# Copies issued from ScalarE, first-product weights in two tiles, and preparation paced by estimated transfers, in a fused attention and expert kernel

## The chip, the cores and the metric

The kernel runs on one core of a Trainium2 chip. The metric is device time in microseconds (us); lower is better. A core has TensorE (PE, the matrix unit, with its weight loads shown apart as PEld), VectorE (DVE), ScalarE (ACT), GpSimd (POOL) and SyncE (SP, which only issues transfers and waits). Each runs its own list of instructions in order. Sixteen DMA engines move the data of all queues; a transfer is issued by an instruction on one engine's list, and if that instruction has to wait, everything behind it on that list waits too.

## The reference

Two blocks follow each other. First a lightning attention over 4 batches, 8 heads, 768 positions and 64 channels, in blocks of 64 positions with a decayed state; then a mixture of 4 experts over the 3072 tokens, all of them dense, with gates that are normalized probabilities.

```python
for b in range(nb):
    intra = np.einsum('bhic,bhjc->bhij', qb, kb) * Dmask[None]
    intra = np.einsum('bhij,bhjd->bhid', intra, vb)
    inter = np.einsum('bhid,bhde->bhie', qb * lam_pow[None], kv_state)
    out[:, :, sl] = intra + inter
    kv_state = lam_block[None, :, None, None] * kv_state + np.einsum('bhsd,bhse->bhde', kb_dec, vb)
...
p = domain_probs / (domain_probs.sum(-1, keepdims=True) + 1e-09)
for e in range(E):            # x is 3072 x 512, w1[e] 512 x 1024, w2[e] 1024 x 512
    h = np.maximum(x @ w1[e], 0.0)
    out += p[:, e:e + 1] * (h @ w2[e])
```

All data is float32.

## The kernel before

**Units and steps.** The tokens are worked in three groups of 1024, each with four experts, so there are twelve units (group, expert), listed in `units`. While the second product (`h @ w2`) of one unit runs, the first product (`x @ w1`) of the next one runs between its parts. Both products use Strassen's scheme with seven products, M1 to M7, in place of eight. In the first product each of the seven is split by the same scheme again, so one outer product consists of seven inner products of 128x256 matmuls. One pass of the inner loop (`for i in range(7)`) is called a step here: one outer product of the first product and one of the second. A step is cut into eight slots, and `now[0]` counts slots over the whole program. From unit 5 on (`NEST`) the second product is split twice too; these steps are called nested.

**Attention** of group 0 runs at the start. That of groups 1 and 2 is put between the steps by `attention`, at slots that `BEGIN` sets, from PSUM banks s0 and s1. The q and k chunks of the last third of the positions are not transposed by PE: they are first copied from DRAM to DRAM into the tensor `across` in 128 copies of 32 KB with rows of 32 floats (`bring_across`, L431 to L444). `trickle` issues one such copy per slot, and `load_more` issues at once what its batch still lacks, and then loads `qx` and `kx` from `across` (`load_across`).

**Weights.** A first product needs for every outer product its block of w1, or a sum of blocks, and the sums of its four quarters: seven pieces of 128x256. GpSimd makes these sums once per expert (`prepare_w1`, `inner_w1`, `inner`; for expert 1 `own_w1`), and SyncE stores the seven pieces, 896 KB, in the DRAM tensor `w1_ops`. For M1, M2 and M4 the block is a plain block of w1 (A11, A12, A22 in `A_OF`); for the other four it is a sum. `feed` (L928) reads the seven pieces back into one tile `ws_in` with a single transfer; two such tiles exist. It is called at the end of slot 0 of a step, of slot 4 in nested steps, for the first product of the next step. The operands of the second product are made alike: `prepare_w2` for units 0 to 4, `prepare_w2_ops` for the nested units, whose pieces go to `w2_ops` and come back in tiles `w2t`.

**What sets the order.** The engines' lists are written out by hand: everything is issued in the order in which this Python program runs. The preparation is a list of small pieces of work, `chores`. At the end of every slot `pump` starts the next one if the planner's clock `free` has come; this clock is pushed on by an estimate of GpSimd's time (`busy`), by a pace per token group (`PACE`), or by 7 slots once `spare` is set, at `NEST`. Stores go through `queue`, which lets them out some slots after the estimated end of their sums. `until` starts chores at once if something due isn't made yet. For each group after the first, `x_fill` loads the transposed activations of one outer product into its slot `xs`; four sums of them follow, on GpSimd (`x_inner`), or on VectorE for the last four of the seven outer products of the last group (`own_x`).

The names that the change and the prediction touch: `tt` L101, `load` L140, `store` L177, `pump` L187, `inner` L211, `prepare_w2_ops` L319, `x_fill` L387, `bring_across` L434, `trickle` L446, `load_across` L454, `feed` L928, `feed2` L1041, `feed3` L1107, `own_w1` L1421, `keep_own` L1438, and the loop over units and slots from L1628 on. Line L102 is the one line that all elementwise operations of VectorE and GpSimd share, L1018 the matmuls of the first product, L1072 and L1371 those of the second product (L1371 nested), L1026 and L1030 ScalarE's copies out of PSUM and its relu in the first product.

Of the kernel before, what the change touches and what calls it, by code (L numbers as in the profile page):

```python
# [21 lines left out]
def kernel(  # L22
# [30 lines left out]
    nc = tc.nc  # L53
# [46 lines left out]

    def tt(eng, o, a, b, op):  # L101
        eng.tensor_tensor(out=o, in0=a, in1=b, op=op)  # L102
        if eng is nc.gpsimd:
            busy[0] = max(busy[0], now[0]) + math.prod(o.shape[1:]) / (640 if spare else 480)
        else:
            vector(math.prod(o.shape[1:]), PSUM in (a.space, b.space))
# [6 lines left out]
    now, busy, free, filled, spare = [0], [0.0], [0.0], [0.0], []  # L113
# [31 lines left out]
    def load(n, names="qkv"):  # L145

        c, b = where(n)
        for name in names:
            x = ({"k": acc_tile, "v": w2_tile} if n < CPG else {}).get(name, small)(f"{name}n")
            src = {"q": q, "k": k, "v": v}[name][b, :, c * C:(c + 1) * C, :]  # L150
            if name == "v":
                to, of = x[:].rearrange("p (h d) -> p h d", d=D), src.rearrange("h p d -> p h d")
                for h in (slice(0, 4), slice(4, 8)) if n < CPG else (slice(0, 8),):
                    nc.sync.dma_start(out=to[:, h], in_=of[:, h])
# [20 lines left out]
    LEFT = 1  # L175
# [10 lines left out]
    def pump(pace=1.0, force=False):  # L186
# [5 lines left out]
        begins = chores and (force or free[0] <= now[0] and not (spare and busy[0] > now[0] + 1))  # L192
        while queue and (force or queue[0][0] <= now[0] or begins and len(queue) > LEFT):
            queue.pop(0)[1]()
        if begins:
            begin = free[0] = max(free[0], now[0] - 1)
            was = max(busy[0], now[0])
            chores.pop(0)()
            free[0] = max(free[0], begin + max(pace * (busy[0] - was), 7 if spare else 1))
# [11 lines left out]
    def inner(eng, what, to, blk, ops, at):  # L211
# [3 lines left out]
        for i, (name, x, y, op) in enumerate(ops):  # L215
            b[name] = s[:, SLOT[name]]
            tt(eng, b[name], b[x], b[y], op)
        store(lambda: (
            nc.sync.dma_start(out=to[:, 0], in_=blk[:, 0, 0:256]),
            nc.sync.dma_start(out=to[:, 1:5], in_=s[:]),  # L220
            nc.sync.dma_start(out=to[:, 5:7], in_=blk[:, 1].rearrange("p (a f) -> p a f", a=2)),
            made.add(what),
        ))
# [27 lines left out]
    def prepare_w1(e):  # L251
        st = {}

        def block(name, i, j):
            t = stage.tile([P, 2, W], FP32, name="w1b", tag="st")
            src = moe_w1[e, j * 256:(j + 1) * 256, i * W:(i + 1) * W]
            nc.sync.dma_start(out=t[:], in_=src.rearrange("(c p) f -> p c f", p=P))
            st[name] = t
# [15 lines left out]
    def prepare_w2(e):  # L274
        st = {}

        def block(name, i, j):
            t = stage.tile([P, 2, 2, DH], FP32, name="w2b", tag="st")
            for uu in range(2):
                for c in (slice(0, 1), slice(1, 2)) if e == 0 else (slice(0, 2),):  # L280
                    nc.sync.dma_start(out=t[:, uu, c], in_=w2_block(e, uu, i, j)[:, c])
            st[name] = t

        def total(name, n, a, b, op):
# [4 lines left out]
                nc.sync.dma_start(out=w2_sums[e, n].rearrange("p u w -> p (u w)"), in_=flat[0]),  # L289
# [17 lines left out]
    def inner_w2(e, m, blk, two):  # L307
# [8 lines left out]
        store(lambda: ([nc.sync.dma_start(out=to[:, x], in_=b[n]) for n, x in at], made.add(("w2", e, m))))  # L316

    def prepare_w2_ops(e, eased):
# [10 lines left out]
        def block(name, i, j):  # L329
            t = st[name] = two("w2b")  # L330
            for q in range(2):
                r = j * W + q * 256
                src = moe_w2[e, r:r + 256, i * DH:(i + 1) * DH]
                nc.sync.dma_start(out=t[q], in_=src.rearrange("(c p) d -> p c d", p=P))
# [53 lines left out]
    def x_fill(g, m):  # L388
# [3 lines left out]
        for a in range(2):  # L392
            nc.sync.dma_start(
# [3 lines left out]
        if g == LAST and SEQ.index(m) >= 3:  # L397
# [9 lines left out]
    def raw_w1(e, name):  # L407
# [6 lines left out]
        for c in range(2):  # L414
            r = j * 256 + c * P
            for f in (slice(0, 256), slice(256, W)) if e == 0 and i == 0 else (slice(0, W),):
                nc.sync.dma_start(out=to[c][:, f], in_=moe_w1[e, r:r + P, i * W:(i + 1) * W][:, f])
# [18 lines left out]
    def bring_across(b):  # L436
        for x, of in enumerate((q, k)):
            for y in range(4):
                for ac in range(NHP):
                    src = of[b, 4 * (y // 2) + ac, SECOND * C:, (y % 2) * 32:(y % 2 + 1) * 32]  # L440
                    to = across[x, y * 32:(y + 1) * 32, ac, b]
                    pieces.append((b, lambda to=to, src=src: nc.sync.dma_start(
                        out=to, in_=src.rearrange("(t p) d -> p t d", p=32),
# [10 lines left out]
    def load_across(n):  # L454
        c, b = where(n)
        for x, name in enumerate("qk"):
            t = small(f"{name}x")
            nc.sync.dma_start(
# [322 lines left out]
    def pair_sums(g, x, o):  # L781
# [3 lines left out]
        for to, a, b in ((0, b12, b11), (1, b22, s[:, 0]), (2, b22, b12), (3, b21, s[:, 1])):  # L785
            tt(nc.gpsimd, s[:, to], a, b, ALU.subtract)
        store(lambda: (
            nc.sync.dma_start(out=x_blocks[g - 1, :, x, 0], in_=b11),
            nc.sync.dma_start(out=x_blocks[g - 1, :, x, 1:3], in_=o[1][:].rearrange("p (i t) -> p i t", i=2)),
            nc.sync.dma_start(out=x_blocks[g - 1, :, x, 3:7], in_=s[:]),  # L790
# [137 lines left out]
    def feed(g, e, m):  # L928
        until(("w1", e, m))
        ws = stream.tile([P, 7, 256], FP32, name="ws_in", tag="w")  # L930
        nc.sync.dma_start(out=ws[:], in_=w1_ops[e, MS.index(m)])
        fed[g, e, m] = {i: ws[:, W1_AT[i]] for i in W1_AT}
# [109 lines left out]
    def feed2(g, e, m):  # L1042
# [3 lines left out]
        for uu in range(2):  # L1046
# [6 lines left out]
            nc.sync.dma_start(out=t[:], in_=src)  # L1053
# [3 lines left out]
    def second_product(g, e, m, banks):  # L1057

        def part(sj, s):
# [31 lines left out]
            if unit_of[g, e] in (E - 1, NEST - 1) and m in ("M2", "M6", "M5", "M3"):  # L1091
                to = rows[n] if g == 0 else partial[n % CPG * P:(n % CPG + 1) * P]
                results.append(lambda: nc.sync.dma_start(out=to[:, j * DH:(j + 1) * DH], in_=o))
# [16 lines left out]
    def feed3(e, m, k):  # L1110
# [3 lines left out]
        if e == FINAL and m != SEQ3[0]:  # L1114

            if k == 0:
                t = xp.tile([P, 7, 256], FP32, name="w2s", tag="x" + SEQ[SEQ3.index(m)])
                if (e, m) == PLAIN:
                    i, j = int(A_OF[m][1]) - 1, int(A_OF[m][2]) - 1
                    src = moe_w2[x_e, j * W:(j + 1) * W, i * DH:(i + 1) * DH]  # L1120
                    nc.sync.dma_start(out=t[:, 0:4], in_=src.rearrange("(k p) d -> p k d", p=P))
                    fed3[e, m, 0] = t
                    return
                nc.sync.dma_start(out=t[:], in_=w2_ops[x_e, MS.index(m)].rearrange("p k c d -> p k (c d)"))
# [5 lines left out]
        nc.sync.dma_start(  # L1130
# [59 lines left out]
    def give(m, t, tags, dds=(0, 1)):  # L1190
# [13 lines left out]
        nc.sync.dma_start(  # L1204
# [62 lines left out]
    def turned_product(t, h, w):  # L1267
# [10 lines left out]
        nc.sync.dma_start(  # L1278
# [12 lines left out]
    def first_result():  # L1291
# [14 lines left out]
        def park(x):  # L1306
            i, j = RESULT[x]
            to = parked[i * DH:(i + 1) * DH, j * W:(j + 1) * W].rearrange("(k p) t -> p k t", k=2)
            nc.sync.dma_start(out=to, in_=sums[x][:].rearrange("p (k t) c -> p k (t c)", k=2))

        def gather(n):
            t, po = small("y"), small("po")
            for b in range(4):
                c = n * P + b * 32
                nc.sync.dma_start(
# [3 lines left out]
            nc.sync.dma_start(out=po[:], in_=partial[n * P:(n + 1) * P])  # L1319
# [7 lines left out]
        def finish_rows(n):  # L1327
            t, po = gathered_out.pop(n)
            tt(nc.gpsimd, t[:], t[:], po[:], ALU.add)
            store(lambda: nc.sync.dma_start(out=rows[CPG + n], in_=t[:]))  # L1330
# [66 lines left out]
    b12.append(stream.tile([P, 7, 256], FP32, name="b12", tag="w"))  # L1397
# [23 lines left out]
    def own_w1(m):  # L1421
# [9 lines left out]
        )))  # L1431
# [5 lines left out]
    def keep_own(what, to, pieces):  # L1437
        return lambda: ([nc.sync.dma_start(out=to[:, x:y], in_=of) for (x, y), of in pieces], made.add(what))  # L1438
# [130 lines left out]
    fill = [(*u, m) for u in units[2:] for m in SEQ]  # L1569
# [59 lines left out]
    PACE = 1.0, 1.4, 1.0  # L1629
    first_steps = first_result()  # L1630
    for at, (g, e) in enumerate(units):
        if at == 0:
            chores.extend(prepare_w2(2) + prepare_w1(3) + prepare_w2(3))
            for x in (2, 3):
                chores.extend(prepare_w2_ops(x, False))
            chores.extend(prepare_w1(0))
            chores.extend(prepare_w2_ops(0, True))
# [6 lines left out]
        if at == NEST - 1:  # L1644
            forget()
        blocks, banks = {}, {}
        for i in range(7):
# [36 lines left out]
            for x, part in enumerate(order):  # L1684
# [31 lines left out]
                if x == (4 if nested else 0) and at * 7 + i >= 6 and fill:  # L1716
# [3 lines left out]
                if x % 2 or at * 7 + i >= 8:  # L1720
# [35 lines left out]
```

## Time and profile before

| | us |
|---|---|
| median of 3 runs | 1188.23 |
| lowest and highest | 1187.45, 1188.76 |
| profiled execution | 1193.83 |
| its span, first to last instruction | 1192.0 |

The page of the profile gives for each engine the time that it was busy, out of that span:

```profile
PE 1155.0 (97%) x8011; PEld 996.4 (84%) x8011; DVE 821.9 (69%) x1504; ACT 316.6 (27%) x638; POOL 802.9 (67%) x764
```

SyncE isn't in that line: issuing a transfer doesn't count as busy. What it does is read from the timeline of its queue (SPq), where each row is one issue or several of one line, with the time of its start and its length. The chain of work that ended last, followed back from the last instruction, is by engine and line:

```profile
PE 78%; DMA 8%; POOL 6%; DVE 5%; issue 2%; SPq 1%; ACT 1%; ACTq 0%; POOLq 0%; DVEq 0%
PE pg L1018 33%; PE pq L1371 20%; PE q L1072 15%; DMA ws_in<-w_ops 6%; POOL acc L102 2%; PE pM L1474 2%; POOL m L102 2%; PE pc L1474 2%; DVE m L102 2%; DVE sums L102 1%; DVE xs L102 1%; PE op L731 1%; PE sp L677 1%; POOL ops L102 1%; PE op L749 1%
```

The largest groups of transfers, with KB each and the median us from issue to landing:

```profile
ws_in<-w_ops SPq DMA_DIRECT2D x70, 896.0 KB, 6.9
w2t<-w_ops SPq DMA_DIRECT2D x129, 256.0 KB, 3.2
w2b<-in_moe_w_dram SPq DMA_DIRECT2D x56, 256.0 KB, 5.0
w_ops<-ops SPq DMA_DIRECT2D x28, 512.0 KB, 4.4
```

In such lines `pg` is the PSUM bank of the first product, `q` and `pq` those of the second, and numbers at the end of names are left out (`w_ops` stands for `w1_ops` and `w2_ops`). A wait is put down to what ended it.

### The profile page before, as it was taken

How to read it: one execution, taken by the hardware profiler on the slowest of the kernel's cores; microseconds unless marked ns; L12 is line 12 of the kernel's file. 1: busy time of each engine (PE TensorE's matmuls, PEld its weight loads, DVE VectorE, ACT ScalarE, POOL GpSimd, SP SyncE). 2: the span in 40 equal slices, each digit the busy share in tenths (PEclk: the TensorE clock that was granted, in tenths of full speed). 3: DMA queues.
4: the chain of work that ended last, by engine and by line, in shares of the span. 5: the costliest groups of instructions: out<-in, count | busy, mean ns of one | idle time of the engine just before them, and what ended most of it. 6: DMA issues, size and time to landing. Idle time of an engine off the chain costs nothing.

```text
span 1192.0 us, 21838 instructions
## 1 busy us (share of the span) xinstructions
PE 1155.0 (97%) x8011; PEld 996.4 (84%) x8011; DVE 821.9 (69%) x1504; ACT 316.6 (27%) x638; POOL 802.9 (67%) x764
## 2 busy tenths in 40 slices
PE   8999999989998899999999999999999999999998
PEld 7788888868777788887888888888888888888887
DVE  4576885568456766874775566798876576777785
ACT  3321122112211121121134242242253342241331
POOL 2846328545554486794689598798599794793894
PEclk9999999999999999999999999999999999999999
DMA  8884667889899999979786767686686967566642
GB/s 185 218 267 143 188 196 221 264 255 271 257 273 290 286 299 318 304 255 319 239 278 216 220 210 243 203 259 197 191 254 214 287 188 213 167 197 179 173 186 71
DMA packets 293994, 273.92 MB, mean 230 GB/s; under 512 B 139840, under 2 KB 240128, under 8 KB 293888
## 3 DMA queue, kind: packets, MB, share of 16 engines
q1 hardware_dynamic: 280096, 268.11, 73.9%
q10 hardware_dynamic: 13792, 4.41, 1.6%
q8 instruction: 64, 1.05, 0.4%
q14 instruction: 42, 0.34, 0.1%
HBM read 194.83 MB, written 81.82 MB: 232 GB/s over the span
## 4 chain that ended last, share of the span: by engine, by line
PE 78%; DMA 8%; POOL 6%; DVE 5%; issue 2%; SPq 1%; ACT 1%; ACTq 0%; POOLq 0%; DVEq 0%
PE pg L1018 33%; PE pq L1371 20%; PE q L1072 15%; DMA ws_in<-w_ops 6%; POOL acc L102 2%; PE pM L1474 2%; POOL m L102 2%; PE pc L1474 2%; DVE m L102 2%; DVE sums L102 1%; DVE xs L102 1%; PE op L731 1%; PE sp L677 1%; POOL ops L102 1%; PE op L749 1%
## 5 line engine op out<-in xcount | busy, mean ns | idle before, releaser
L1018 PE MATMUL pg<-xs,ws_in 128*128 128x256 f32 x1960 | 479.5, 385 | 21.7 <-DMA ws_in<-w_ops 18.8
L1018 PEld LDWEIGHTS pg<-xs,ws_in 128*128 128x128 f32 x1960 | 371.6, 192 | 80.8 <-issue 15.7
L102 DVE TENSOR_TENSOR m<-pg,m 128x512 f32<-128x512 f32 x451 | 308.0, 687 | 142.6 <-PE pg L1018 130.9
L1072 PE MATMUL q<-w2t,m 128*128 128x256 f32 x1120 | 267.0, 381 | 0.5 <-DVE m L102 0.5
L1072 PEld LDWEIGHTS q<-w2t,m 128*128 128x128 f32 x1120 | 214.4, 192 | 31.1 <-DVE m L102 1.2
L102 POOL TENSOR_TENSOR m<-m,decay 128x512 f32<-128x512 f32 x112 | 141.2, 1279 | 76.7 <-ACT m L1030 66.4
L1371 PE MATMUL pq<-acc,w2t 128*128 128x256 f32 x688 | 169.5, 379 | 0.2 <-POOL m L102 0.2
L102 DVE TENSOR_TENSOR sums<-pq,sums 128x256 f32<-128x256 f32 x272 | 113.1, 420 | 72.5 <-PE pq L1371 59.9
L1371 PEld LDWEIGHTS pq<-acc,w2t 128*128 128x128 f32 x688 | 130.4, 190 | 18.8 <-issue 0.5
L1030 ACT ACTIVATE m<-m 128x512 f32<-128x512 f32 x132 | 82.8, 630 | 203.6 <-DVE m L102 192.1
L102 DVE TENSOR_TENSOR m<-m,m 128x512 f32<-128x512 f32 x112 | 98.1, 876 | 7.2 <-ACT m L1030 7.2
L1026 ACT COPY m<-pg 128x512 f32<-128x512 f32 x88 | 51.5, 586 | 148.1 <-PE pg L1018 134.3
L1090 DVE SCALAR_TENSOR_TENSOR acc<-q,gate,acc 128x256 f32<-128x256 f32 x108 | 51.8, 480 | 55.0 <-PE q L1072 54.7
L102 POOL TENSOR_TENSOR acc<-hT,hT 128x512 f32<-128x512 f32 x56 | 70.4, 1274 | 13.3 <-PE pq L1371 13.3
L102 POOL TENSOR_TENSOR w2o<-w2b 128x512 f32<-128x512 f32 x28 | 38.9, 1411 | 55.0 <-DMA w2b<-in_moe_w_dram 17.5
L102 POOL TENSOR_TENSOR acc<-hT,acc 128x512 f32<-128x512 f32 x56 | 71.3, 1274 | 4.9 <-PE pq L1371 0.9
L1371 PE MATMUL pq<-hT,w2t 128*128 128x256 f32 x288 | 74.0, 379 | 0.1
L950 ACT COPY up<-m 128x512 f32<-128x512 f32 x56 | 32.5, 588 | 131.2 <-DVE m L102 131.0
L102 POOL TENSOR_TENSOR xs<-xs 128x256 f32<-128x256 f32 x40 | 31.6, 790 | 44.9 <-DMA xs<-x_blocks 42.5
L1371 PEld LDWEIGHTS pq<-hT,w2t 128*128 128x128 f32 x288 | 54.6, 190 | 7.9 <-DVE sums L102 0.5
L882 ACT COPY hp<-m 128x512 f32<-128x512 f32 x84 | 48.4, 589 | 43.3 <-POOL m L102 21.7
L1371 PE MATMUL pq<-m,w2t 128*128 128x256 f32 x228 | 58.5, 380 | 0.1
(140 smaller groups left out, 1350.7 us busy)
## 6 DMA issues: line engine op xcount, KB each, us to landing
ws_in<-w_ops SPq DMA_DIRECT2D x70, 896.0 KB, 6.9
w2t<-w_ops SPq DMA_DIRECT2D x129, 256.0 KB, 3.2
w2b<-in_moe_w_dram SPq DMA_DIRECT2D x56, 256.0 KB, 5.0
w_ops<-ops SPq DMA_DIRECT2D x28, 512.0 KB, 4.4
w2t<-w_sums SPq DMA_DIRECT2D x40, 256.0 KB, 4.1
w_sums<-w2o SPq DMA_DIRECT2D x16, 512.0 KB, 4.8
w2t<-in_moe_w_dram SPq DMA_DIRECT2D x30, 256.0 KB, 4.5
xs<-x_blocks SPq DMA_DIRECT2D x28, 256.0 KB, 4.9
```

Source lines behind the costliest of these rows:

```text
L102: eng.tensor_tensor(out=o, in0=a, in1=b, op=op)
L677: nc.tensor.matmul(out=sp[r][half[x], ac * BL:(ac + 1) * BL], lhsT=hc(kT)[half[r], ac, blk[x]], rhs=hc(qT)[half[r], ac, blk[x]], start=(ac ...
L731: nc.tensor.matmul(out=op[r][half[y], cols(a, r) if x == r else apart(a)], lhsT=state[half[r], x, 2 * a + y], rhs=by_block(qs)[half[r], 2 ...
L882: nc.scalar.copy(out=there[x][:], in_=blk[at][:])
L950: nc.scalar.copy(out=there[at][:], in_=a[at][:])
L1018: nc.tensor.matmul(out=p[:, j * 256:(j + 1) * 256], lhsT=ws[i][:, j * P:(j + 1) * P], rhs=xs[i], start=(fresh and j == 0), stop=True, skip ...
L1026: nc.scalar.copy(out=new[at][:], in_=p[:])
L1030: nc.scalar.activation(out=new[at][:], in_=new[at][:], func=AF.Relu)
L1072: nc.tensor.matmul(out=p[:, s * DH:(s + 1) * DH], lhsT=h[A_OF[m]][:, c * 256 + s * P:c * 256 + (s + 1) * P], rhs=fed2[g, e, m][uu][:, c], ...
L1090: nc.vector.scalar_tensor_tensor(out=o, in0=x, scalar=w, in1=o, op0=ALU.mult, op1=ALU.add)
L1371: nc.tensor.matmul(out=p[:, 0:256], lhsT=fed3[e, m, x // 2][:, x % 2, c * P:(c + 1) * P], rhs=b[B_OF[i]][:, c * 256:(c + 1) * 256], start= ...
L1474: nc.tensor.matmul(out=p[:, s * 256:(s + 1) * 256], lhsT=a[c][:, f:f + P], rhs=b[:, c, j * 256:(j + 1) * 256], start=(s == 0 and c == 0 an ...
```

## The change

All transfers but a few now go through a helper, `send`, which keeps two estimates in slots: until when the DMA engines are occupied (`moved`, from the size and the packet length), and until when SyncE is issuing (`asked`, 0.27 slot for each). Five things use it or come with it.

1. The 128 copies into `across` are issued by ScalarE (`by=nc.scalar`). `trickle` is called in the odd slots, and in slot 4 from step 4 on (five a step), where it was called in every slot from step 8 on.
2. `feed` fills two tiles, with three and four of the seven pieces. Each kind has two buffers. From step 14 on they are issued in slots 1 and 5 (2 and 5 in nested steps); step 13 issues three, so that from then on the second tile comes one step, and the first one two steps, ahead of its use.
3. Where the block is a plain one, only the four sums are stored in `w1_ops`; `feed` reads the other three pieces from w1 itself, so that it takes two transfers for a tile.
4. `pump` starts a chore only if `moved` and `asked` are less than 4 slots (`FULL`) ahead. The pace of group 1 is 1.0 instead of 1.4; a chore after `NEST` takes 5 slots instead of 7 while more than 13 are left. The operands of the second product of expert 3 are prepared after w1 of expert 0, one step later in the list, and with small tiles.
5. In the last group the activations' sums of all seven outer products are made on VectorE.

```diff
+    def send(out, in_, by=None):
+        n = 4 * min(packet(out), packet(in_))
+        moved[0] = max(moved[0], now[0]) + 4 * math.prod(out.shape) / n * (9 + n / 25) / 16 / 1714
+        if by is None:
+            asked[0] = max(asked[0], now[0]) + 0.27
+        (by or nc.sync).dma_start(out=out, in_=in_)
...
-        begins = chores and (force or free[0] <= now[0] and not (spare and busy[0] > now[0] + 1))
+        begins = chores and (
+            force or free[0] <= now[0] and max(moved[0], asked[0]) < now[0] + FULL
+            and not (packed and busy[0] > now[0] + 1)
+        )
...
-            free[0] = max(free[0], begin + max(pace * (busy[0] - was), 7 if spare else 1))
+            free[0] = max(free[0], begin + max(pace * (busy[0] - was), (5 if len(chores) > 13 else 7) if spare else 1))
...
-            nc.sync.dma_start(out=to[:, 0], in_=blk[:, 0, 0:256]),
-            nc.sync.dma_start(out=to[:, 1:5], in_=s[:]),
-            nc.sync.dma_start(out=to[:, 5:7], in_=blk[:, 1].rearrange("p (a f) -> p a f", a=2)),
+        pieces = [(to[:, 1:5], s[:])]
+        if A_OF[what[2]][0] == "S":
+            pieces += [(to[:, 0], blk[:, 0, 0:256]), (to[:, 5:7], blk[:, 1].rearrange("p (a f) -> p a f", a=2))]
+        store(lambda: ([send(out=x, in_=y) for x, y in pieces], made.add(what)))
...
-        if g == LAST and SEQ.index(m) >= 3:
+        if g == LAST:
             own_x(m, g, 6)
...
-                    pieces.append((b, lambda to=to, src=src: nc.sync.dma_start(
-                        out=to, in_=src.rearrange("(t p) d -> p t d", p=32),
+                    pieces.append((b, lambda to=to, src=src: send(
+                        out=to, in_=src.rearrange("(t p) d -> p t d", p=32), by=nc.scalar,
...
-    def feed(g, e, m):
+    def feed(g, e, m, part):
         until(("w1", e, m))
-        ws = stream.tile([P, 7, 256], FP32, name="ws_in", tag="w")
-        nc.sync.dma_start(out=ws[:], in_=w1_ops[e, MS.index(m)])
-        fed[g, e, m] = {i: ws[:, W1_AT[i]] for i in W1_AT}
+        x, y = ((0, 3), (3, 7))[part]
+        ws = stream.tile([P, y - x, 256], FP32, name="ws_in", tag="w" + "ab"[part])
+        a = A_OF[m]
+        if a[0] == "A":
+            i, j = int(a[1]) - 1, int(a[2]) - 1
+            src = moe_w1[e, j * 256 + part * P:j * 256 + (part + 1) * P, i * W:i * W + (256, W)[part]]
+            if part == 0:
+                send(out=ws[:, 0], in_=src)
+                send(out=ws[:, 1:3], in_=w1_ops[e, MS.index(m), :, 1:3])
+            else:
+                send(out=ws[:, 0:2], in_=w1_ops[e, MS.index(m), :, 3:5])
+                send(out=ws[:, 2:4].rearrange("p a f -> p (a f)"), in_=src)
+        else:
+            send(out=ws[:], in_=w1_ops[e, MS.index(m), :, x:y])
+        fed.setdefault((g, e, m), {}).update({i: ws[:, n - x] for i, n in W1_AT.items() if x <= n < y})
...
-    fill = [(*u, m) for u in units[2:] for m in SEQ]
+    fill = [(*u, m, part) for u in units[2:] for m in SEQ for part in range(2)]
...
-    PACE = 1.0, 1.4, 1.0
+    PACE = 1.0, 1.0, 1.0
+    FEED = (1, 5), (2, 5)
...
             chores.extend(prepare_w2(2) + prepare_w1(3) + prepare_w2(3))
-            for x in (2, 3):
-                chores.extend(prepare_w2_ops(x, False))
-            chores.extend(prepare_w1(0))
-            chores.extend(prepare_w2_ops(0, True))
+            chores.extend(prepare_w2_ops(2, False) + prepare_w1(0))
+            for x in (3, 0):
+                chores.extend(prepare_w2_ops(x, True))
...
         if at == NEST - 1:
             forget()
+            packed.append(True)
...
-                if x == (4 if nested else 0) and at * 7 + i >= 6 and fill:
+                if fill and at * 7 + i >= 6 and x in ((0, 1) if at * 7 + i < 13 else (1, 3, 5) if at * 7 + i == 13 else FEED[nested]):
                     feed(*fill.pop(0))
...
-                if x % 2 or at * 7 + i >= 8:
+                if x % 2 or x == 4 and at * 7 + i >= 4:
                     trickle()
```

In the rest of the diff `nc.sync.dma_start` becomes `send`, and the tile `b12` takes the shape of a second tile.

## The prediction

> **What bounds the kernel now.** I read the page's busy shares first: TensorE (PE) 97% of a span of 1192.0 us, VectorE 69%, GpSimd 67%, ScalarE 27%. So only PE's idle time and slow time can be won. Next the view of waits, for PE:
>
> ```profile
> PE pg L1018 <- DMA ws_in<-w_ops: 18.8, 10, 4.4
> PE pg L1018 <- DVE m L102: 3.7, 8, 1.1
> ```
>
> One cause stands out: ten late weight tiles of the first product. A table by stretches says where:
>
> ```profile
> 100.00:200.00 100.00, 98.24 (x814) 84.84 (x813) 76.32 (x137) 19.70 (x41) 46.74 (x52) 1.00 0.68 204
> 200.00:420.00 220.00, 201.40 (x1862) 170.90 (x1862) 139.28 (x249) 37.27 (x84) 111.08 (x119) 0.97 0.90 269
> 420.00:560.00 140.00, 138.66 (x1149) 119.53 (x1141) 91.24 (x159) 25.55 (x57) 101.95 (x119) 1.00 0.96 299
> ```
>
> (Start:end, length, then busy us and count of PE, weight loads, VectorE, ScalarE, GpSimd; granted clock, DMA share, GB/s.) PE loses 18.6 us between 200 and 420, and its clock is 0.97 there. Between 420 and 560 it loses 1.3 us with the DMA engines busier. The timeline shows both halves of the price, the wait and the slow matmuls after it:
>
> ```profile
> 363.03 2.59 PE L1018 MATMUL pg<-xs,ws_in 128*128 128x256 f32 x8 [3.08 <-DMA ws_in<-w_ops]
> 365.41 3.00 PE L1072 MATMUL q<-w2t,m 128*128 128x256 f32 x8
> 438.20 1.89 PE L1018 MATMUL pg<-xs,ws_in 128*128 128x256 f32 x8
> ```
>
> Eight undisturbed matmuls take 1.89 (1.97 after a short wait). After the five waits over 2 us the rows of eight read 3.34, 3.61, 2.59, 3.48 and 2.76 (excess over 1.97: 5.9 in all), and two rows behind them 3.00 and 2.83 (over 1.89: 2.1). So lateness costs 18.8 + 8.0 = 26.8 us.
>
> Why late? SyncE's timeline before the tile that landed at 362.9:
>
> ```profile
> 353.17 1.90 SPq L442 DMA_DIRECT2D across<-in_q_dram  x2
> 355.17 2.26 SPq L1053 DMA_DIRECT2D w2t<-in_moe_w_dram  x2
> 357.52 0.42 SPq L931 DMA_DIRECT2D ws_in<-w_ops  x1
> 358.00 0.56 SPq L442 DMA_DIRECT2D across<-in_q_dram  x1
> ```
>
> No gap: it waits for nothing, it is still issuing. The loop puts this feed at the end of a step's first slot, which PE passed at 349.4; SyncE is 8 us behind. From 328.1 to 342.0 its rows add up to 12.8 of 13.9 us. Feeds issued between 250 and 400 precede their first matmul by 5.5 to 9.7 us and land in 6.9 (median); in steps of 600 to 1130, where SyncE has time, most precede it by 12 to 13.7. SyncE's issuing is the bound, in 200 to 420 and again near 530 to 560.
>
> **The change, part by part.**
>
> *Copies to ScalarE.*
>
> ```profile
> L442 SPq DMA_DIRECT2D across<-in_q_dram x64: 551/609/2673, 60.8 to 366.4; - x64
> L442 SPq DMA_DIRECT2D across<-in_k_dram x64: 550/609/2558, 108.8 to 402.1; - x64
> DMA to landing us min/median/max: 2.1/4.5/7.8
> ```
>
> Of these 128, 90 lie in 200 to 420: 90 x 0.609 = 55 of SyncE's 220 us. There the split adds 26 feed issues x 0.382 = 10. Counted in the built programs between the matmuls of 200 and 425, SyncE has 275 issues before and 198 after, ScalarE 67. At 0.64 each (the 20 issues of those 12.8 us) 198 make 127 of 225 us, 56%. Its timeline from 100 to 200 sums to 55%, and no feed or load made PE wait there.
>
> *Two tiles per weight set.* Before, a feed stands eight slots ahead of its use (end of slot 0 to slot 1 of the next step). A step without attention is 60 matmul rows x 0.216 = 13.0 us, a slot 1.62, so 13 us. After, tile a goes out in slot 5 for slot 1 two steps on (11 slots, 17.8 us), tile b in slot 1 or 2 for slot 3 of the next step (at least 8 of 1.51, the slot of a nested step: 12 us). Landing 896 KB takes 6.9, 512 KB w1 loads 7.1 to 7.9: slack 4 to 10 us where it was below nothing. Together with the copies I take 24 of the 26.8 (bounds 7, if the engines are the limit, and 26.8). With SyncE caught up, one more PE us goes: 0.31 + 0.79 near 256, where ScalarE had waited 4.65 for a late x_blocks store. The 130 further issues (70 feeds become 200) and 86 further waits on PE cost nothing: in this trace 287 matmuls have a separate wait ahead, with a median excess of 0. Without that cover, 130 x 0.38 = 50 us on SyncE, where its queue is full.
>
> *Plain blocks not stored.* 24 store issues and 12 x 384 KB, 4.7 of 273.92 MB, go. Reading 1 KB rows instead of 7 KB rows takes some back. By itself 0; it is part of the slack.
>
> *The last copies come in one run.* Copies go five a step now instead of eight, so 16 are left when chunk 21 needs them, and ScalarE's program has 17 in a row (slots 1 and 2 of step 21) ahead of a PSUM copy. Before:
>
> ```profile
> 433.23 0.59 ACT L1026 COPY m<-pg 128x512 f32<-128x512 f32 x1 [0.28 <-PE pg L1018]
> 435.82 0.59 ACT L1026 COPY m<-pg 128x512 f32<-128x512 f32 x1 [2.00 <-PE pg L1018]
> 444.01 0.59 ACT L1026 COPY m<-pg 128x512 f32<-128x512 f32 x1 [7.61 <-PE pg L1018]
> ```
>
> The second of these ends at 436.4 and the matmul at 438.20 (shown above) must wait for it. After, ScalarE starts the run at 433.8. Lower bound: 17 x 0.39 (ScalarE's median issue, L1657) = 6.6, the copy ends at 441.0, PE stands 2.8 us. Upper: the built program gives both queues eight completion counters in turn, so the 9th copy waits for the 1st to land (4.5) and the 17th for the 9th: about 10.2, the copy ends at 444.6, PE stands 6.4. I take 5, nearer the upper end, since these 32 KB land no sooner (4.5) than 128 KB w1 loads (4.6), plus 8.0/5 = 1.6 of slow clock: +6.6. SyncE's qx load waits for the same copies, so SyncE stands some 13 us; w2t loads there precede their use by 17 us or more, the next tile a by 17.8.
>
> *x sums on VectorE, w2 operands of expert 3 later.* 12 subtractions x 0.797 (38.2/48) = 9.6 us move from GpSimd to VectorE, two thirds into 750 to 775:
>
> ```profile
> 750.00:775.00 25.00, 25.00 (x117) 22.00 (x117) 18.02 (x34) 4.88 (x8) 18.62 (x20) 1.00 0.65 194
> 775.00:800.00 25.00, 24.26 (x112) 20.46 (x110) 23.50 (x41) 10.37 (x18) 24.61 (x20) 1.00 0.81 267
> ```
>
> VectorE gets to 24 of 25 us in the first; in the second, at 23.50, PE lost 0.74. I take +1.5 (bounds 0 and 4). GpSimd gains the operands of expert 3 in 580 to 700; over 625 to 800 its program grows from 151 to 161 us of 175. The tightest due is M3 of expert 0, stored 3 us ahead of its load instead of 10: +1 (0 to 4).
>
> *Pacing* moves loads and sums, and forces none early that wasn't forced before: 0.
>
> **Sum:** -24 - 1 + 6.6 + 1.5 + 1 = -15.9. The profiled execution took 1193.83 (span 1192.0), 5.6 over the median 1188.23; off its span the sum gives 1176.1, off the median **1172**. Own range 1162 (run of copies harmless) to 1180.
>
> **A rule against it.** The row first: SyncE's rows fill 12.8 of 13.9 us. The Trainium skill, "DMA: Bandwidth & Descriptors", section "Issuing engines are not separate DMA queues", says that all queues end in the same 16 engines and that issuing from several engines saves only the sequencer's issue time, usually small beside the transfer. By it the 25 us are not won and the 9.1 of new costs stay: 1197. The row decides for me: here the issue time is the queue.
>
> **Rivals.**
>
> *The DMA engines are the bound* (15%). Share 0.90 over 220 us is 198 us of packets. If 0.93 is all they give, the stretch stays 213: 7 won there and 4 later, 9.1 paid: 1186. For: 0.96 follows at once. Against: at that 0.96 PE lost 1.3 of 140 us, and the program moves 58 MB instead of 61 in the stretch.
>
> *ScalarE gets stuck behind SyncE* (18%; slower). Each copy waits for the DMA eight places back over both queues. 265 issues in 225 us put that 6.8 us back; landing takes 4.5, so 2.3 us of SyncE lag are free, and a PSUM copy has 1.8 us more (436.4 to 438.2). It decides from a lag of 4 us. At 5 each of the 16 PSUM copies in the four M1 and M5 steps of the stretch stands 0.9: 14 us, and the feeds win only 15: -15 + 14 + 9.1 = +8, **1196**. For: the lag is 8 now, and qx loads make SyncE wait for ScalarE in turn. Against: at 56% busy SyncE should run level, as it does in 100 to 200.
>
> *The stretch 700 to 800 gives it back* (9%): GpSimd at 92% and VectorE at 97% lose the upper bounds 4 + 4, and late operands as much again: 1172 - 2.5 + 16 = 1185.
>
> **How the numbers follow.** Forecast 58%, rivals as given. 0.2% (2.4 us) is about what this kernel's measurement tells from none. Faster: 58 + 10 of the first rival + 7 of the last = 75. Same: 4 + 2 + 1 = 7. Slower: 16 of the second + 1 + 1 = 18. Range: 1158 is all 27.8 won at no cost (1160.4), less 2 for the spread of runs; 1195 leaves out half of the slower case.
>
> **What would show it.** Right: PE's wait for ws_in under 4 us; granted clock 1.00 in 200 to 420; a PE gap of 3 to 6 us near 420 to 440, ended by a ScalarE copy behind a row of L114 issues; PE at 24.0 to 24.8 of 25 where 750 to 800 now lies. Wrong: ws_in waits of 10 us or more with SyncE idle (engines), or many waits of PE for "ACT m" (second rival).

## The result and the profile after

| | before | after |
|---|---|---|
| median, us (runs, lowest to highest) | 1188.23 (5; 1184.14 to 1191.5) | 1175.06 (5; 1173.13 to 1178.2) |
| profiled span, us | 1192.0 | 1176.4 |
| issues of SyncE in 200 to 425 (built program) | 275 | 198 |

The ratio is 0.9895, with a 95% interval of 0.9866 to 0.9924: the changed kernel is about 1% faster. The wait that was to go went, and the new one that was foretold came, somewhat larger. The view of PE's waits after:

```profile
PE pg L1047 <- ACT m L1055: 7.2, 1, 7.2
PE pg L1047 <- DVE m L117: 5.8, 10, 1.4
PE pq L1400 <- DMA w2t<-w_ops: 1.3, 1, 1.3
```

Columns: who waited for whom, us in total, times, longest. No first product waits for `ws_in` any more; 18.8 us stood there before. One single wait of 7.2 us for a ScalarE copy is now the largest. The table by stretches (PE, weight loads, VectorE, ScalarE, GpSimd; clock, DMA share, GB/s) shows both; the last two rows cover the work that stood at 750 to 800 before, which comes some 14.6 us earlier now:

```profile
200.00:420.00 220.00, 213.84 (x2018) 183.03 (x2016) 149.37 (x266) 42.41 (x98) 131.08 (x140) 1.00 0.94 279
420.00:560.00 140.00, 135.77 (x1052) 117.62 (x1053) 87.96 (x155) 22.55 (x49) 80.96 (x92) 0.98 0.87 277
735.00:760.00 25.00, 23.36 (x107) 19.49 (x106) 21.58 (x38) 4.05 (x7) 20.64 (x19) 1.00 1.03 333
760.00:785.00 25.00, 23.99 (x110) 20.34 (x109) 23.43 (x40) 10.60 (x19) 24.61 (x21) 1.00 0.92 287
```

From 200 to 420 PE worked 213.84 us of 220 (201.40 before) at a clock of 1.00 (0.97), with the DMA engines busier than before, 0.94. The loss moved to the edge of the next stretch. The timeline of the changed kernel there, PE's rows first, then ScalarE's, then SyncE's (start, length, what; in brackets the idle time before it and what ended it):

```profile
415.16 1.89 PE L1101 MATMUL q<-w2t,m 128*128 128x256 f32 x8
424.23 3.78 PE L1047 MATMUL pg<-xs,ws_in 128*128 128x256 f32 x8 [7.18 <-ACT m L1055]
427.80 2.25 PE L1101 MATMUL q<-w2t,m 128*128 128x256 f32 x8
...
412.51 11.04 ACTq L114 DMA_DIRECT2D across<-in_k_dram  x16
423.59 0.59 ACT L1055 COPY m<-pg 128x512 f32<-128x512 f32 x1 [11.10 <-DMA across<-in_k_dram]
...
408.77 0.38 SPq L114 DMA_DIRECT2D ws_in<-w_ops  x1
416.10 0.52 SPq L114 DMA_DIRECT2D qx<-across  x1
425.30 0.52 SPq L114 DMA_DIRECT2D kx<-across  x1
```

ScalarE issues copies for 11 us (these 16, and one more just ahead of them), the PSUM copy behind them ends at 424.2, PE stands 7.18 us and then runs two rows at less than full speed (3.78 in place of 1.97, 2.25 in place of 1.89): 9.4 us in all. SyncE stands too, with its `qx` and `kx` loads waiting for the same copies, but PE waits for none of its loads there.

### The profile page after: what moved, and what is told of

Read it like the earlier page. It is cut to its first block, busy times and chain, and to the rows that moved or that the text cites. A ratio compares the mean times of both kernels' runs of the same rounds, so it can differ in the third digit from the quotient of the medians.

```text
span 1176.4 us, 21932 instructions
## 1 busy us (share of the span) xinstructions
PE 1148.0 (98%) x8011; PEld 992.5 (84%) x8011; DVE 828.1 (70%) x1516; ACT 316.8 (27%) x638; POOL 796.5 (68%) x752
## 4 chain that ended last, share of the span: by engine, by line
PE 84%; DMA 5%; DVE 5%; POOL 2%; issue 1%; SPq 1%; ACTq 1%; ACT 1%; POOLq 0%; DVEq 0%
PE pg L1047 35%; PE pq L1400 21%; PE q L1101 18%; PE pM L1503 2%; DMA ws_in<-w_ops 2%; DVE m L117 2%; PE pc L1503 2%; DVE xs L117 1%; DVE sums L117 1%; PE sp L694 1%; PE sp L701 1%; PE op L748 1%; DMA decay<-gate_rows 1%; PE op L766 1%; PE qp L664 1%
## 5 line engine op out<-in xcount | busy, mean ns | idle before, releaser
L1047 PEld LDWEIGHTS pg<-xs,ws_in 128*128 128x128 f32 x1960 | 369.2, 190 | 69.0 <-DVE m L117 11.2
L117 POOL TENSOR_TENSOR w2o<-w2b 128x512 f32<-128x512 f32 x26 | 34.6, 1350 | 41.8 <-DMA w2b<-in_moe_w_dram 24.3
L117 POOL TENSOR_TENSOR acc<-m,acc 128x512 f32<-128x512 f32 x38 | 48.4, 1274 | 5.3 <-DMA partial<-acc 2.5
```

The costliest lines, as they stand in the source:

```text
L1047: nc.tensor.matmul(out=p[:, j * 256:(j + 1) * 256], lhsT=ws[i][:, j * P:(j + 1) * P], rhs=xs[i], start=(fresh and j == 0), stop=True, skip ...
```

## The experiments

Each kernel is the changed one with one edit, except the third, which is the kernel before with one edit. Each was timed beside runs of the kernel before on the same chip. Some texts speak of the loss of PE in a stretch of 100 us (a bucket): for every 128x256 matmul, what the next matmul's start lies behind its own beyond 216 ns, summed from the trace where it is over 60 ns. Waits and slow matmuls are in it together, waits right behind one of attention's 64x64 matmuls are not.

| kernel | median, us | ratio to before, 95% interval | span | loss 300 to 400 |
|---|---|---|---|---|
| after | 1175.06 | 0.9866 to 0.9924 | 1176.4 | 5.7 |
| e1_spread | 1169.74 | 0.9825 to 0.988 | 1168.1 | 7.7 |
| e2_sync | 1173.34 | 0.9845 to 0.9901 | 1172.5 | 2.1 |
| e3_before_scalar | 1175.73 | 0.9878 to 0.9926 | 1172.8 | 12.5 |
| e4_old_lead | 1173.74 | 0.9859 to 0.9906 | 1174.4 | 4.6 |
| e5_sync_spread | 1174.80 | 0.9868 to 0.9919 | 1172.4 | 11.6 |
| e8_half | 1175.97 | 0.9868 to 0.9923 | 1171.0 | 11.2 |
| e9_early_act | 1170.44 | 0.9826 to 0.988 | 1166.4 | 2.7 |
| e9_early_sync | 1171.02 | 0.9816 to 0.9877 | 1172.2 | 2.9 |
| e6_own_x | 1185.39 | 0.997 to 1.0005 | 1183.8 | 2.5 |
| e7_order | 1185.16 | 0.9957 to 0.9993 | 1183.7 | 4.2 |
| e11_plain | 1183.84 | 0.9945 to 0.9978 | 1182.7 | 5.5 |
| e10_pacing | 1173.32 | 0.9866 to 0.9903 | 1170.0 | 3.0 |

**Is the stall at 417 the run of 17 copies?** (e1_spread)

```diff
-                if x % 2 or x == 4 and at * 7 + i >= 4:
+                if x % 2 or at * 7 + i >= 8:
                     trickle()
```

> The changed kernel with the copies let out one a slot from step 8 on, as before, so that the run of 17 copies ahead of the PSUM copy m21 in step 21 is gone (the longest run left is 10, near 230 us, ahead of no PSUM copy that PE waits for soon). Theory (the run cost a wait of 7.2 us and about 2 us of half-speed matmuls): no wait of PE for ScalarE over 2 us, 1166 us (1164 to 1169). Rival (more copies a step keep ScalarE on its completion counters, so the stall moves to several smaller ones between 220 and 400): 1172 to 1180, with waits of PE for m by ScalarE that sum to 5 us or more.

The stall of 7.2 is gone; two waits for ScalarE are left, 3.2 us together, the longest 1.8. In its timeline the PSUM copies of the same step wait for PE alone:

```profile
414.90 0.59 ACT L1055 COPY m<-pg 128x512 f32<-128x512 f32 x1 [0.28 <-PE pg L1047]
417.49 0.59 ACT L1055 COPY m<-pg 128x512 f32<-128x512 f32 x1 [2.00 <-PE pg L1047]
```

The span falls by 8.3 us, the median by 5.3 (to 1169.7, 0.7 over the expected range), and no run of it (highest 1172.26) is as slow as the fastest of the changed kernel (1173.13), though the two were not timed side by side. So the run is the cause, and the other kernels that keep it on ScalarE (e4, e6, e7, e10, e11) keep a stall of 7.0 to 8.3 us. Some of what it cost comes back in 300 to 400, where the loss grows from 5.7 to 7.7.

**Which part removed the lateness?** One kernel takes the move to ScalarE out, one has it alone, one takes the longer lead out.

```diff
# e2_sync
-                        out=to, in_=src.rearrange("(t p) d -> p t d", p=32), by=nc.scalar,
+                        out=to, in_=src.rearrange("(t p) d -> p t d", p=32),
# e3_before_scalar, on the kernel before
-                    pieces.append((b, lambda to=to, src=src: nc.sync.dma_start(
+                    pieces.append((b, lambda to=to, src=src: nc.scalar.dma_start(
# e4_old_lead
-                if fill and at * 7 + i >= 6 and x in ((0, 1) if ... else FEED[nested]):
-                    feed(*fill.pop(0))
+                if fill and at * 7 + i >= 6 and x == (4 if nested else 0):
+                    feed(*fill.pop(0))
+                    feed(*fill.pop(0))
```

> The changed kernel with the 128 copies issued by SyncE again; everything else as changed. Theory (SyncE's issuing was the bound, and both parts give slack): SyncE has some 265 issues of 0.64 us in 225 us again, 75% or more, and the run of 17 stands in its list; the stall of 9 us behind ScalarE is gone, 3 to 12 us of lateness of ws_in come back: 1170 to 1182. Rival A (the longer lead alone removes all the lateness): 1166, PE's wait for ws_in under 1 us. Rival B (the move to ScalarE alone matters): 1185 or more, ws_in waits of 12 us or more.

> The kernel before with only the issuer of the 128 copies changed, from SyncE to ScalarE; one copy a slot as before, weights in one tile with the old lead. Theory (SyncE's issuing alone made the feeds late): ws_in waits fall from 18.8 to under 4 us, no run of 17 copies, 1163 to 1168, faster than the changed kernel. Rival (landing under load needs the longer lead): ws_in waits of 8 us or more, 1175 to 1185.

> The changed kernel with both tiles of a weight set fed together at the slot of before (end of slot 0, of slot 4 in nested steps). Theory (SyncE's queue alone made the feeds late, the lead is a reserve): within 3 us of the changed kernel, 1173 to 1179, ws_in waits under 3 us. Rival (the lead carries the gain): ws_in waits of 8 us or more, 1183 to 1192.

Either the move or the other parts take most of the lateness away by themselves. With the move taken out (e2; the lead, the plain blocks, the pacing and five copies a step stay) PE worked 99.92 of the 100 us between 300 and 400, and 3.9 us of `ws_in` waits are left, 3.5 of them after the run of copies, which now stands in SyncE's list:

```profile
414.38 11.09 SPq L114 DMA_DIRECT2D across<-in_k_dram  x16
...
437.95 3.61 PE L1047 MATMUL pg<-xs,ws_in 128*128 128x256 f32 x8 [3.45 <-DMA ws_in<-w_ops]
```

The median of e2, 1173.3, and its waits lie where they were expected. The lead alone, on the kernel before, was not run. With the copies alone (e3) a single wait of 0.3 us for `ws_in` is left, and the median is that of the whole change, 1175.73. But I had expected 1163 to 1168, and its loss in 300 to 400 is 12.5. One event makes some two thirds of it, 5.9 us of wait and 2.8 of slow matmuls in the two PE rows (ScalarE, SyncE, VectorE, PE):

```profile
367.77 1.85 ACTq L442 DMA_DIRECT2D across<-in_k_dram  x2
369.66 0.63 ACT L1030 ACTIVATE m<-m 128x512 f32<-128x512 f32 x1 [8.71 <-issue]
...
361.27 6.18 SPq L334 DMA_DIRECT2D w2b<-in_moe_w_dram  x6
...
370.33 0.69 DVE L102 TENSOR_TENSOR m<-m,m 128x512 f32<-128x512 f32 x1 [9.24 <-ACT m L1030]
...
373.06 3.78 PE L1018 MATMUL pg<-xs,ws_in 128*128 128x256 f32 x8 [5.91 <-DVE m L102]
376.63 2.85 PE L1072 MATMUL q<-w2t,m 128*128 128x256 f32 x8
```

Between the copy that ScalarE began to issue at 358.20 and the next, at 367.77, only relus ran. In the built program that next copy waits for the completion counter of the `w2b` load which SyncE issued at 361.27, 6.7 us after PE had passed its place in the program; it landed after 6.5 us, at 367.75. The relu behind the copies held VectorE for 9.24 us and PE for 5.91. This is the mechanism of the second rival, ScalarE stuck behind SyncE, in a kernel whose SyncE still lags by 6 to 8 us. In e4 (everything but the longer lead) it doesn't show: as expected, it equals the changed kernel, with the same stall for ScalarE (7.1) and no wait for `ws_in` in the list.

**How should the copies be spread?** Four kernels set the pace and the issuer of the copies:

```diff
# e5_sync_spread: one a slot from step 8, all from SyncE
+                if x % 2 or at * 7 + i >= 8:
# e8_half: the same, in turn from ScalarE and SyncE
+                if x % 2 or at * 7 + i >= 8:
+                        ... by=(nc.scalar, None)[ac % 2],
# e9_early_act: one a slot up to step 8, then four a step, from ScalarE; e9_early_sync: from SyncE
+                if x % 2 or at * 7 + i < 9:
```

> The changed kernel with the 128 copies issued by SyncE as before and one a slot as before, so that neither ScalarE nor a run of 17 stands in the way; the longer lead, the plain blocks and the pacing stay. Theory (two remedies, each enough by itself: with 17.8 us of lead SyncE may lag by 8 us): ws_in waits under 2 us in all, no wait of PE for ScalarE over 1 us, 1164 to 1168. Rival (SyncE's issuing binds whatever the lead, the lag grows until PE waits): ws_in waits of 6 us or more in 200 to 420, 1172 to 1180.

> The changed kernel with one copy a slot, in turn from ScalarE and from SyncE, so that no two copies follow each other on ScalarE without a slot between them. Theory (ScalarE is stuck in proportion to its copies in a row, 17 in step 21 cost 9 us, up to 10 in a row cost 1 to 3 us near 367 when every copy is ScalarE's): no wait of PE for ScalarE over 0.5 us, loss of PE in 300 to 400 under 3 us, 1164 to 1167, the lowest of the kernels so far. Rival (mixing both queues makes ScalarE wait for SyncE's late transfers all the same): waits of PE for m by ScalarE or by VectorE behind ScalarE of 3 us or more, 1170 to 1175.

> The changed kernel with the copies turned round in time: one a slot up to step 8, four a step from step 9 on (the changed kernel has four a step up to step 3 and five from step 4), all from ScalarE; none is left to be brought in one run in step 21, and the longest run is 9, near 120 us. Theory (the rate of copies in 300 to 400 is what costs there: 5 a step lost 5.7 us in that bucket, 8 a step 7.7, and 11 to 12 in two kernels that issue some or all from SyncE; the run of 17 cost 9): loss of PE in 300 to 400 under 5 us, no wait for ScalarE over 2 us, 1164 to 1168. Rival (the losses in 300 to 400 come from something else that the faster stretch of copies doesn't touch, and the copies at 100 to 200 push attention's copies on ScalarE): 1169 to 1174.

> The same order of copies, one a slot up to step 8 and four a step after it, but issued by SyncE. Theory (with the long lead and few copies in 300 to 400 it is of no account which engine issues them): ws_in waits under 1.5 us, 1163 to 1168, within 2 us of the kernel that issues them from ScalarE. Rival (the move to ScalarE is needed in itself): ws_in waits of 4 us or more, 1172 or more.

Both expectations for one copy a slot from step 8 on missed: e5 and e8 came out at 1174.8 and 1176.0, not at 1164 to 1168, each with some 4 us of `ws_in` waits and a wait of 2.7 for VectorE near 398. The rows trace that last wait back to SyncE too. VectorE stands for a store of `x_blocks` that e5 issues at 392.88 and the changed kernel at 381.83 (the changed kernel's row first, then e5's):

```profile
381.83 1.68 SPq L114 DMA_DIRECT2D x_blocks<-xc  x2
...
392.88 1.37 SPq L114 DMA_DIRECT2D x_blocks<-xc  x2
398.61 1.04 DVE L117 TENSOR_TENSOR qs<-qx,decay 128x512 f32<-128x512 f32 x1 [3.36 <-DMA x_blocks<-xc]
```

So the lead doesn't cover every lag, and half the copies on each engine is no cure. In e1, whose copies are all ScalarE's, the longest wait of the stretch (2.2 us, near 368) is of the other kind: a relu behind copies held VectorE for 5.2 us.

With the copies one a slot from step 8 on, four kernels can be set side by side: neither remedy (before) 1188, the move to ScalarE alone (e3) 1175.7, all the other parts without it (e5) 1174.8, both (e1) 1169.7. Each gives 12 to 13 us alone, and the second still adds 5 to 6. No run of e1 (highest 1172.26) is as slow as the fastest of e3 (1174.14) or e5 (1173.16).

What sorts the kernels in 300 to 400 is the pace there. With eight copies a step the loss there is 7.7 to 12.5, whoever issues them (e1, e3, e5, e8); with five 2.1 to 5.7 (after, e2, e4, e6, e7, e10, e11); with four 2.7 and 2.9. These are single profiles, and the lowest of the first group is only 2.0 above the highest of the second. The line of 300 to 400 for e9_early_act, below, has 99.36 us of PE; the changed kernel has 97.00 there.

```profile
300.00:400.00 100.00, 99.36 (x951) 85.41 (x950) 73.62 (x131) 16.92 (x39) 57.04 (x61) 1.00 0.95 291
```

The medians of e9_early_act and e9_early_sync, 1170.4 and 1171.0, miss the expected 1168 by 2 to 3 us: the SyncE kernel loses 8.3 us in 200 to 300 instead (one wait of 4.5 for a relu of ScalarE near 249, on whose list a copy had stood 6.4 us for a late store of `x_blocks`), and its `ws_in` wait of 1.7 is a little over the bound. That the issuer is of no account with the copies turned round held, within 0.6 us. These two and e1 cannot be told apart by their intervals; all three are faster than before by about 1.5%.

**Are the small parts small?** Four kernels undo one each: the x sums, the order, the plain blocks, the pacing.

```diff
# e6_own_x
-        if g == LAST:
+        if g == LAST and SEQ.index(m) >= 3:
# e7_order
-            chores.extend(prepare_w2_ops(2, False) + prepare_w1(0))
-            for x in (3, 0):
-                chores.extend(prepare_w2_ops(x, True))
+            for x in (2, 3):
+                chores.extend(prepare_w2_ops(x, False))
+            chores.extend(prepare_w1(0))
+            chores.extend(prepare_w2_ops(0, True))
# e11_plain (and the same in own_w1)
-        if A_OF[what[2]][0] == "S":
+        if True:
...
-        if a[0] == "A":
+        if False:
# e10_pacing
-            force or free[0] <= now[0] and max(moved[0], asked[0]) < now[0] + FULL
-            and not (packed and busy[0] > now[0] + 1)
+            force or free[0] <= now[0] and not (spare and busy[0] > now[0] + 1)
...
-    PACE = 1.0, 1.0, 1.0
+    PACE = 1.0, 1.4, 1.0
```

(e10 also has 7 in place of `5 if len(chores) > 13 else 7`.)

> The changed kernel with the sums of x for the first three outer products of the last group on GpSimd again. Theory (12 more subtractions fill VectorE near 750 to 785, and PE waits there for m): the waits of PE for VectorE in 735 to 800, 2.4 us of excess in the changed kernel, fall to 1.2 or less; 1173 to 1175. Rival (those waits come from the step's other work, not from the subtractions): the same waits within 0.5 us, 1175 to 1177.

> The changed kernel with the preparation in the order of before (operands of the second product for expert 3 ahead of the first product's weights for expert 0, and not eased). Theory (the 1.3 us wait for a w2t near 738 comes from expert 3's operands being made later): that wait is gone, 1173 to 1176. Rival (it is a matter of the load's place in SyncE's queue): the wait stays, within 0.3 us, and the time too.

> The changed kernel with the plain w1 blocks stored in w1_ops again and the two tiles of every weight set fed from there with one transfer each: 24 store issues and 4.7 MB come back, 48 feed issues go. Theory (this part costs and gains nothing by itself, there is slack on both sides): 1173 to 1178, waits of ws_in none. Rival (the stores of 384 KB that come back delay sums or feeds in 300 to 400, where the DMA share is 0.94): 1179 to 1183.

> The changed kernel with the planner's pacing of before (no limit by estimated transfers or issues, a pace of 1.4 for the second token group, 7 slots between pieces of preparation in the nested steps, the guard on GpSimd's backlog only there); copies, tiles, plain blocks, order and x sums as changed. Theory (three other parts undone one by one each made one operand of the second product late, 8 to 10 us; with 7 slots instead of 5 between pieces the same operands are stored later still): a wait of PE for w2t of 4 us or more between 600 and 800, 1180 to 1190. Rival (what the prediction said, the pacing forces nothing early and is worth nothing): 1173 to 1178, no wait for w2t over 2 us.

All four theories missed, and e10 came out as its rival had it. The other three are the finding of the study. Against the changed kernel, which was timed in another round, undoing the x sums costs 10.3 us of the median, the order 10.1, the plain blocks 8.8; in the spans of the profiled executions it is 7.4, 7.3 and 6.3. Each time one w2t load comes late by 4.6 to 10.2 us, once (e11 has a second wait, of 1.7 near 908). The clearest is e11, SyncE's rows, then GpSimd's, then PE's:

```profile
776.98 0.37 SPq L114 DMA_DIRECT2D w_ops<-w2o  x1
788.94 0.32 SPq L114 DMA_DIRECT2D w_ops<-ops  x1
...
794.22 0.42 SPq L114 DMA_DIRECT2D w2t<-w_ops  x1
...
786.69 1.42 POOL L117 TENSOR_TENSOR ops<-w2o 128x256 f32<-128x256 f32 x2
788.19 0.72 POOL L117 TENSOR_TENSOR ops<-ops,w2o 128x256 f32<-128x256 f32 x1
...
798.85 1.40 PE L1400 MATMUL pq<-m,w2t 128*128 128x256 f32 x4 [4.61 <-DMA w2t<-w_ops]
```

SyncE stands from 777.4 to 788.9 at a store whose sum GpSimd makes at 786.7 to 788.9; the load of w2t behind it goes out at 794.2 and PE waits 4.6 us. In e6 the same happens in the same place, and PE waits longer:

```profile
789.58 0.32 SPq L114 DMA_DIRECT2D w_ops<-ops  x1
794.11 0.42 SPq L114 DMA_DIRECT2D w2t<-w_ops  x1
...
799.53 2.07 PE L1400 MATMUL pq<-m,w2t 128*128 128x256 f32 x4 [7.88 <-DMA w2t<-w_ops]
```

The operand is M3 of expert 0, which the prediction had named as the tightest. Counted in the built programs, the matmuls issued between its store and its load are 22 before, 7 after, 3 in e6, 5 in e11, 60 in e10. In e7 another one is hit, 175 us earlier: the wait for w2t is 10.2 us, ended at 624.7, behind a store of w1 sums that SyncE reached at 607.6 and issued at 613.67.

```profile
607.23 0.32 SPq L114 DMA_DIRECT2D partial<-acc  x1
613.67 0.32 SPq L114 DMA_DIRECT2D w_ops<-ops  x1
...
619.45 1.41 SPq L114 DMA_DIRECT2D w2t<-w_ops  x3
```

There the first product's weights for expert 0 are prepared later than in the changed kernel, as before, but the two-tile feed asks for them earlier. Building these programs shows what ties the three together: `until` has to start work at once for something due, in e6 and e11 for this M3 (slot 451), in e7 for M4 of the first product's weights of expert 0 (slot 337), and in the kernel before, the changed one and e10 for nothing after slot 122. So the store goes on SyncE's list at once, ahead of its sum. e10, the pacing undone, was as fast as the changed kernel (1173.3), had no wait for w2t in its list, and stored that operand earlier: the pacing uses up the reserve which the x sums and the plain blocks then have to give back. That e11 makes the sum later because more estimated transfers hold the planner back fits that, and its program forces two weights of expert 3 as well (slots 163 and 175), but no run took the limit alone out of e11.

## Why the prediction was right, by its own steps

| step | foretold, us | measured | from |
|---|---|---|---|
| lateness of `ws_in` gone | -24 (7 to 26.8) | -26.8 | no such wait of a first product, clock 1.00 |
| run of copies | +6.6 (stall 2.8 to 6.4, taken 5) | +9.4 (stall 7.2) | rows at 424.23 and 427.80; e1's span falls by 8.3 |
| x sums on VectorE | +1.5 (0 to 4) | 0 | e6: loss of PE to VectorE in 735 to 800 2.2 without, 2.4 with |
| operands made later | +1 (0 to 4) | +1.3 | wait for w2t at 738 |
| late store near 256 | -1 | -1.1 | waits of 0.31 and 0.79 gone |
| plain blocks, pacing | 0 | 0 in the sum | but see below |
| not foretold | | +3.7 | waits for VectorE's m 3.7 to 5.8; attention before 120: 1.4 for GpSimd and 1.1 with no cause shown are new, 0.9 for VectorE gone |
| sum on the span | -15.9 | -15.6 | 1192.0 to 1176.4 |

The rows above add up to -13.5; the other 2.1 us were not traced to a row. In the foretold sum the run of copies was 2.8 too small and the lateness 2.8 too small as well, so the sum is better than its terms, and that is luck. These spans are one execution each, the changed kernel's being the slowest of its five; by the medians the gain is 13.2 us, 2.7 less than the sum, and 1175 was measured where 1172 was forecast.

**What bounded the kernel** was read rightly in the main: SyncE's issuing. In 200 to 425 its rows took 189 of 225 us before and take 119 now (53%; foretold 56%), and the lateness went although the DMA share rose to 0.94. The first rival, that the DMA engines are the bound at 0.93, falls with that and with e2 and e3 (in e2 PE worked 99.92 of the 100 us in 300 to 400 at a share of 0.95). "It waits for nothing" was too strong, though. The view of what SyncE waited for in 353 to 358, before:

```profile
SPq L1053 <- PE q L1072: 1.6, 1, 1.6
```

One of the two `w2t` issues right ahead of the late feed stood 1.6 us until PE released its buffer; a row of the timeline holds such a wait as well as the issuing.

The Trainium skill, "DMA: Bandwidth & Descriptors", section "Issuing engines are not separate DMA queues", says that a second issuing engine saves only the time to issue, usually small beside the transfer. For one copy this trace agrees (0.609 us to issue, 4.5 to land). What doesn't follow, for this kernel, is that little is saved: the list was full of such issues, and changing only the issuer (e3) gave 1.0%. The section's other half, that the transfers share the same engines, is not spoken against by any run here.

**The mis-sized term** is the run of copies. The place, the chain and the sign were right, the stall 7.2 in place of 5, above the upper bound of 6.4. What failed is the price of one issue on ScalarE: I took 0.39, the median of another ScalarE issue, for the lower end, and let waits for completion counters make the upper one. The view of line L114 on ScalarE from 411 to 424:

```profile
L114 ACTq DMA_DIRECT2D across<-in_k_dram x16: 557/622/951, 412.5 to 422.9; - x16
...
DMA to landing us min/median/max: 2.1/2.3/4.2
```

The first line gives minimum, median and maximum in ns. The issue itself takes 0.622 us, as on SyncE (0.609), and the copies land in 2.3 us, so that nearly all found the counter of the transfer eight places back free (one waited 0.27 us, for a `ws_in` load of SyncE); 16 took 11.04 from ScalarE here and 11.09 from SyncE in e2. The nearer row, the same transfer on the other engine, was in the prediction: 17 x 0.609 + 0.59 from 433.8 would have given 444.7 and a stall of 6.5. The slow matmuls behind the stall cost 2.2, where 1.6 was taken.

**The second rival**, ScalarE behind SyncE, was held off by the price named for it: SyncE ran level. e3 shows that it is real where SyncE lags 6 to 8 us, over the 4 us from which it was to decide. But it came as one large hit of 8.7 us in a stretch that lost 12.5, instead of sixteen small ones that make 14.

**The third rival**, the stretch 700 to 800, didn't come, but was less far off than the text had it. PE has 23.36 and 23.99 of 25 us there, a little under the foretold 24.0 to 24.8, with the 1.3 us wait for w2t in the first. The prediction costed the x sums, the plain blocks and the order as small losses or nothing; they are the cover of M3 of expert 0 and of the weights for expert 0, and without any one of them 9 to 10 us of the median are lost. "By itself 0; it is part of the slack" was right for the sum and hid the price of that slack, which the text owed.

So the gain of the whole change, 13 us of the median, is no larger than that of its first part alone (e3). The rest adds 6.0 us to that part while the copies keep their old pace (e1), and the new pace, which made the run of copies, takes 5.3 of them back.

## What to carry to other kernels

Price a moved issue by the same transfer's issue on its old engine, since its cost went with the transfer, and then look for the longest run of such issues ahead of anything that PE waits for. A fast change can be a set of parts that protect each other: a part that adds nothing to the sum may be what keeps one load from standing behind an unready store, so undo the parts one by one before calling any of them idle. Two remedies for the same lateness don't add up: here 12 and 13 us alone made 18 together. Copies without a near due date can be issued where the queue is less full: one a slot before step 9 and four a step behind it, they made no run and left 2.7 to 2.9 us of loss in 300 to 400, though the time was no better than e1's.

## What was not expected of the hardware

One engine's issues can wait for another engine's late transfers: in e3 a ScalarE copy waited 6.8 us (360.95 to 367.77) until a SyncE load issued at 361.27 had landed, because the built program gives both queues the same eight completion counters in turn. Why eight copies a step cost 7.7 to 12.5 us in 300 to 400, where five or four cost 2.1 to 5.7, is settled only event by event: that one in e3, a relu behind copies in e1, SyncE's late loads and stores in e5 and e8. Whether the copies' small packets, the issuing or the counters make SyncE and ScalarE so late there stays open.
